# A swapped and negated third row in the table of a Fourier step, and one copy out of PSUM in place of three

## The chip, the cores and the metric

The kernel runs on one core of one Trainium2 chip. Its engines are TensorE (PE in the profile, its weight loads PEld), VectorE (DVE), ScalarE (ACT), GpSimd (POOL) and SyncE (SP, which here only issues DMAs). Each works through its own queue in order. The metric is the time of one launch on the device in microseconds; the median of three runs of the kernel before is 3733.18 us (3731.57 to 3733.58).

## The reference

Two blocks in a row, all in float32. The first is a long convolution, done with Fourier transforms, between two gates:

```python
h_filt = (np.maximum(pos_emb @ w1, 0.0) @ w2) * np.exp(-0.01 * pos)[:, None]
u = x * v                                             # x, v: (4, 12480, 128)
Uf = np.fft.rfft(u, n=2 * S, axis=1)
Hf = np.fft.rfft(h_filt, n=2 * S, axis=0)
y = np.fft.irfft(Uf * Hf[None], n=2 * S, axis=1)[:, :S, :]
x2 = (x * y).reshape(B * S, D)                        # 49920 x 128
```

The second is a layer whose activation is h cos(h):

```python
h = x2 @ w_in                                         # 49920 x 2048
out = (h * np.cos(h)) @ w_out                         # 49920 x 128
```

## The kernel before

The transform of each of the four batches is made of small matrix products, in two steps there (f1, f2) and two back (i1, i2). A sequence is laid out as 104 rows (partitions) by 120 columns, and the columns are folded first: sums of mirrored columns go to places 0 to 59, differences to places 64 to 123. So one column of a pair of channels, called b (64 of them, CB), is a block of 104 partitions by 124 places (KE = 124, ODD = 64).

The first step f1 multiplies this block, as the left operand, with the table c1 (two rows of 96 numbers, a sine and a cosine, of 104 partitions): `f1_mm`, L414 to L417. It does so for each of the two channels i of b, into one PSUM bank of 124 partitions, 2 x 192 numbers each. Partitions 0 to 63 (sums) then hold real and imaginary part in that order. For partitions 64 to 123 (differences) the second transform step wants the two exchanged, and one of them negated. This is done as the results leave PSUM, `f1_evict`, L428 to L435: one copy for partitions 0 to 63 (L431), one copy for the other half's second part (L433), and a negating copy for its first part (the lambdas at L423 and L425). `f1_takers` gives a column b as a whole to ACT or to DVE, by a share. The same step of the filter has its own eviction in five instructions (L437 to L448), since its results go to two tiles.

`units` (L535) drives every step: for each j it calls the matmuls, in two halves, and between the halves takes one `next` of the eviction of the column before. It yields a number of steps, by which the later batches are paced.

The stages, in order of time:

- From 0 to about 64 us: the hidden layer of the filter, and x times v of the first batch (`first_u`: L404 multiplies, L410 sums, on DVE and POOL; the loads L385 go through SP's queue).
- From 64 to 122: f1 of the filter with the eviction `f1_evict_filter`, share 0.53, beside the rest of `first_u` (L895 to L897), then beside `inverse_tables` (L900 to L905): POOL computes arguments (L209 to L226), ACT makes sines of them (L235). These sines lie in ACT's queue between the evictions.
- From 118 to 171: f1 of the first batch, share 0.55 (L922), beside the conversion of w_in (L145 to L168).
- From 171 to 270: f2 of the first batch and the filter at once (`f2_both_units`): ACT and DVE make each table w (L300, L302), PE multiplies, ACT scales the filter's result (L635), which is stored to DRAM (hd).
- Then i1 of the first batch, and from 338 us the main loop (L995 to L1024). It carries the second block tile by tile, 16 chunks c a tile: `moe_up` (PE into "ph", then L755 on ACT and L756 on DVE), `moe_act` (L761 on ACT, L762 on DVE), `moe_sums` on POOL, `moe_down` (L787 on PE). In each chunk `convolve` (L989) pulls as many units of the convolution as it is owed. So i2 of one batch and f1, f2 and i1 of the next, `forward_units` (L713), are woven between the chunks. A tile's begin needs a transposed tile: `moe_turn` (L738) takes one bank for it (PE L136, copied by ACT L744); `moe_back` (L811) transposes results (copied by L818).

In the first part the convolution has eight PSUM banks ("ps"). In the main loop it has two and then three ("cv"), which `moe_turn` shares; "ph" has three, the accumulators two. From the main loop on every matmul with a left operand over 64 columns is cut in two, `tiled` in `mm` (L129 to L132): results for partitions 0 to 63 and from 64 are two instructions, which the profile shows as 104*64 and 104*60. Before that it is one, 104*124. A float32 matmul stands in the trace as two passes, each with its weight load.

Of the kernel before, what the change touches and what calls it, by code (L numbers as in the profile page):

```python
# [9 lines left out]
F32 = mybir.dt.float32  # L10
I32 = mybir.dt.int32
U32 = mybir.dt.uint32
AF = mybir.ActivationFunctionType
ALU = mybir.AluOpType
# [19 lines left out]
def kernel(  # L34
# [46 lines left out]
    nc = tc.nc  # L81
# [4 lines left out]
    N1, N2 = 96, 120  # L86
    R = S // N2
# [3 lines left out]
    ODD = 64  # L91
    KE = ODD + H
# [4 lines left out]
    KF = N1 - 2 * (N2 - N1)  # L97
# [22 lines left out]
    twd = dram.tile([N1, 2, N2], F32, name="twd")  # L120

    const = ctx.enter_context(tc.tile_pool(name="const", bufs=1))
    c1 = const.tile([R, 2, N1], F32, name="c1")
    even = const.tile([KE, 2, N2], F32, name="even")
    tw_w = const.tile([KE, 2, N1], F32, name="tw_w")

# [2 lines left out]
    def mm(dst, left, right, start=True, stop=True):  # L129
        n = dst.shape[0]  # L130
        for lo, hi in ((0, CB), (CB, n)) if tiled[0] else ((0, n),):
            nc.tensor.matmul(dst[lo:hi], left[:, lo:hi], right, start=start, stop=stop)  # L132
# [104 lines left out]
    def forward_tables(pool):  # L237
        t = Tables(pool, nc.vector, 1)
        part = t.whole([P, 1], [[1, 1]], channel_multiplier=1, name="part")
        step = t.whole([P, P], [[1, P]], name="step")  # L240
        step4 = t.whole([P, P], [[4, P]], base=1, name="step4")


        odd_p = t.whole([P, 1], [[1, 1]], base=1, channel_multiplier=2, name="odd_p")
        quarter_p = pool.tile([P, 2], F32, name="quarter_p")
        nc.vector.tensor_scalar(out=quarter_p[:, 0:1], in0=part[:, :], scalar1=float(ODD),
                                scalar2=None, op0=ALU.is_ge)
        nc.vector.scalar_tensor_tensor(
            out=odd_p[:, :], in0=quarter_p[:, 0:1], scalar=-2.0 * ODD, in1=odd_p[:, :],
            op0=ALU.mult, op1=ALU.add)  # L250

        nc.vector.tensor_scalar(out=quarter_p[:, 0:1], in0=quarter_p[:, 0:1],
                                scalar1=-N2 / 2.0, scalar2=N2 / 2.0, op0=ALU.mult, op1=ALU.add)
        nc.vector.tensor_scalar(out=quarter_p[:, 1:2], in0=quarter_p[:, 0:1],
                                scalar1=N2 / 2.0, scalar2=None, op0=ALU.add)
        yield from t.sines(step4, part, 4 * N1, [(c1[:, 0, :], 1), (c1[:, 1, :], 0)])
        yield from t.sines(step, odd_p, 2 * N2,
                           [(even[:, i, :], quarter_p[0:KE, i:i + 1]) for i in range(2)])
        yield from t.sines(step4, odd_p, 2 * TURN, [(tw_w[:, 0, :], 1), (tw_w[:, 1, :], 0)])
# [153 lines left out]

    def f1_mm(ps, u, b, i):  # L414

        mm(ps[0:KE, i * 2 * N1:(i + 1) * 2 * N1], u[:, b, 0:KE, i],
           c1[0:u.shape[0], :, :].rearrange("p r k -> p (r k)"))  # L417

    def f1_takers(b, share):


        if int((b + 1) * share) > int(b * share):
            return nc.scalar.copy, lambda out, in_: nc.scalar.activation(  # L423
                out, in_, AF.Copy, scale=-1.0)
        return nc.vector.tensor_copy, lambda out, in_: nc.vector.tensor_scalar(  # L425
            out=out, in0=in_, scalar1=-1.0, scalar2=None, op0=ALU.mult)

    def f1_evict(ps, b, share):  # L428
        copy, negated = f1_takers(b, share)
        pj = ps[:, 0:4 * N1].rearrange("p (i r k) -> p r k i", i=2, r=2)  # L430
        copy(out=parts[0:ODD, :, :, b, :], in_=pj[0:ODD])  # L431
        yield
        copy(out=parts[ODD:KE, 0, :, b, :], in_=pj[ODD:KE, 1])  # L433
        negated(parts[ODD:KE, 1, :, b, :], pj[ODD:KE, 0])
        yield  # L435

    def f1_evict_filter(ps, b, share):  # L437

        copy, negated = f1_takers(b, share)
        pj = ps[:, 0:4 * N1].rearrange("p (i k) -> p k i", i=2)  # L440
        near, far = ftile[:, b, :, :], above[:, b, :, :]
        copy(out=near[0:ODD], in_=pj[0:ODD, 0:N1 + KF])
        copy(out=far[0:ODD], in_=pj[0:ODD, N1 + KF:])
        yield
        copy(out=near[ODD:KE, 0:N1], in_=pj[ODD:KE, N1:])
        negated(near[ODD:KE, N1:], pj[ODD:KE, 0:KF])
        negated(far[ODD:KE], pj[ODD:KE, KF:N1])
        yield  # L448

    def f2_mm(ps, w, k1, i, filt=False):  # L450
# [84 lines left out]
    def units(n, steps, before, mm, after, parts, ahead=2, skip=0):  # L535


        for j in range(min(ahead, n)):
            for _ in before(j) or ():
                pass  # L540
        yield 0.0
        last = iter(())
        for j in range(n):
            early = iter(before(j + ahead) or () if j + ahead < n else ())
            now = None
            for i in range(parts):
                if i == skip or 2 * (i - skip) == max(parts, 2):
                    now = mm(j, now, int(i > skip))
                if i == 0 and parts == 1:
                    now = mm(j, now, 1)  # L550
                next(last, None)
                next(early, None)
                yield steps / parts
            for _ in early:
                pass
            next(last, None)
            last = after(j, now)
        for _ in last:
            pass
        yield REST  # L560
# [23 lines left out]
            yield from units(H // UA, U_STEPS, before, lambda j, ps, i: None, after, 3,  # L584
                             ahead=bufs - 2)

    def f1_units(bank, u, share=0.5, evict=f1_evict):
        def mm(j, ps, i):
            if i == 0:
                ps = bank()  # L590
            f1_mm(ps, u, j, i)
            return ps

        return units(CB, F1_STEPS, lambda j: None, mm, lambda j, ps: evict(ps, j, share), 2)

    def f2_units(bank):
        with tc.tile_pool(name="there", bufs=3) as pool:
            ws, hs = {}, {}

            def before(j):  # L600
                ws[j] = pool.tile([KE, 2, N2], F32, name="w")
                nc.sync.dma_start(ws[j][:, :, :], wd[j, :, :, :])
                hs[j] = pool.tile([N2, 2, CB, 4], F32, name="h")
                nc.sync.dma_start(hs[j][:, :, :, :], hd[j, :, :, :, :])

            def mm(j, ps, i):
                if i == 0:
                    ps = bank()
                f2_mm(ps, ws[j], 2 * j, i)
                return ps  # L610

            yield from units(N1 // 2, F2_STEPS, before, mm,
                             lambda j, ps: f2_product(pool, ps, hs.pop(j), 2 * j, False), 4)
# [28 lines left out]
    def i1_units(bank):  # L642
        with tc.tile_pool(name="mid", bufs=2) as pool:
            def mm(j, ps, i):
                if i == 0:
                    ps = bank()
                i1_mm(ps, j, i)
                return ps

            yield from units(CB, I1_STEPS, lambda j: None, mm,  # L650
                             lambda j, ps: i1_evict(pool, ps, j), 2)
# [61 lines left out]
    def forward_units(bank, back):  # L713

        f2 = f2_units(bank)
        next(f2)
        yield from f1_units(bank, slots[0:R, :, :, :])
        yield from f2
        next(back)
        yield from i1_units(bank)  # L720
# [114 lines left out]
    with tc.manual_schedule():  # L835
        with tc.tile_pool(name="psum", bufs=8, space=PSUM) as psum, \
                ExitStack() as first:
            def bank():
                return psum.tile([P, BANK], F32, name="ps")

            spool = ctx.enter_context(tc.tile_pool(name="slots", bufs=1))
            slots = spool.tile([P, CB, 2 * N2, 2], F32, name="slots")
            parts = slots[:, :, 0:2 * N1, :].rearrange("p b (r k) i -> p r k b i", r=2)
            above = slots[:, :, 2 * N1:2 * N2, :]
# [6 lines left out]
            with tc.tile_pool(name="layers", bufs=1, side="right") as pool:  # L851
# [16 lines left out]
                window = filter_window(pool)  # L868
                nc.gpsimd.memset(aT[:, 0:H, NCH * ROWS:FR], 0.0)
                sines = forward_tables(pool)  # L870
                peTs = {}
                for i in range(NCH + 1):
# [14 lines left out]
            ftile = fpool.tile([P, CB, N1 + KF, 2], F32, name="ftile")  # L887
            clear_gap(ftile[0:FR, :, :, :])
            with tc.tile_pool(name="out", bufs=1, side="right") as pool:
                for j in range(H // 2):  # L890
                    filter_out(pool, bank, aT, ftile, j, w2_sb)
                    for _ in range(1 + (j % 3 == 0)):
                        next(first_u)
            f1 = f1_units(bank, ftile[0:FR, :, :, :], 0.53, f1_evict_filter)
            for _ in first_u:  # L895
                for _ in range(2):
# [14 lines left out]
            def beside(units, pieces, factor, more=lambda pool: iter(())):  # L911
                with tc.tile_pool(name="convert", bufs=1) as pool:
# [6 lines left out]
                    for _ in [*convert, *other]:  # L919
                        pass  # L920

            beside(f1_units(bank, slots[0:R, :, :, :], 0.55),  # L922
                   [(wind[:, c], w) for c, w in in_pieces], INV_TWO_PI)
            lpool = ctx.enter_context(tc.tile_pool(name="late", bufs=1))
# [130 lines left out]
```

## Time and profile before

| what | value |
|---|---|
| median of the three runs | 3733.18 us |
| span of the profiled execution, first to last instruction | 3730.7 us |
| its own time beyond the span | not recorded; the median of the runs is 2.4 us over the span |
| PE busy, mean granted TensorE clock | 3627.8 us (97%), 0.993 |
| DVE, ACT, POOL busy | 2970.8, 2256.0, 2787.4 us |
| DMA moved | 279.61 MB, mean 75 GB/s |
| f1 matmuls, later batches | 768 of 104*64 and 768 of 104*60 |
| f1 matmuls, first batch and filter | 256 of 104*124 and 256 of 96*124 |
| f1 evictions, later batches | 96 columns on ACT, 96 on DVE, three instructions each |
| f1 evictions, first batch | 35 on ACT, 29 on DVE, three instructions each |
| f1 evictions, filter | 33 on ACT, 31 on DVE, five instructions each |

How to read the lines below. A line of the timeline has the start in us from the span's begin, how long the merged instructions last together, the engine, the line of the code, the operation, output and inputs by tile name, partitions by elements, and how many; in brackets, how long the engine had been idle and which instruction's end released it. A line of the waits has who waited for whom, the sum in us, how often, and the longest. A line of the stretches has the length, then busy us of PE, PEld, DVE, ACT and POOL with the number of instructions, then the granted clock, the DMA share and GB/s. A matmul's duration covers its way through the array, so the next one starts before it ends: pitch is read from starts.

### The profile page before, as it was taken

What the parts mean: (1) busy time and instruction counts of PE and PEld (TensorE: products, weight loads), DVE (VectorE), ACT (ScalarE), POOL (GpSimd) and SP (SyncE); (2) the same over time, 40 slices, a digit from 0 to 9 for tenths busy, and PEclk for the clock granted to TensorE, in tenths of its full rate; (3) what the DMA queues carried; (4) which work ended last, traced back from release to release, by engine and by line L of the source; (5) the groups of instructions that cost most, each with busy time, mean ns of one, the idle gap of its engine ahead of it and who ended that gap; (6) DMA issues with size and microseconds to landing.
All of it is one profiled execution on the core that took longest, in us unless ns stands there. A gap on an engine that the chain in (4) does not pass through costs nothing.

```text
span 3730.7 us, 101448 instructions
## 1 busy us (share of the span) xinstructions
PE 3627.8 (97%) x40298; PEld 2574.6 (69%) x40298; DVE 2970.8 (80%) x5812; ACT 2256.0 (60%) x4660; POOL 2787.4 (75%) x3271
## 2 busy tenths in 40 slices
PE   7898999999999999999999999999999999999999
PEld 6777776666668776766667776666667786666666
DVE  8887887788887777888887777888887757787777
ACT  5756666665554556665555455665565446666666
POOL 7666987578883887588884788578885447887877
PEclk9999999999999999999999999999999999999999
DMA  6263551012221662022210563012220261000000
GB/s 168 62 182 101 162 157 56 15 53 72 71 62 45 164 172 57 13 63 70 73 55 16 152 171 98 19 38 73 73 64 25 73 175 31 19 19 24 19 24 14
DMA packets 209710, 279.61 MB, mean 75 GB/s; under 512 B 17111, under 2 KB 146535, under 8 KB 209111
## 3 DMA queue, kind: packets, MB, share of 16 engines
q1 hardware_dynamic: 209239, 273.12, 26.0%
q8 instruction: 321, 5.26, 0.6%
q14 instruction: 150, 1.23, 0.1%
HBM read 193.64 MB, written 79.42 MB: 73 GB/s over the span
## 4 chain that ended last, share of the span: by engine, by line
PE 83%; DVE 4%; ACT 1%; POOL 1%; issue 1%; DMA 0%; ACTq 0%; POOLq 0%; DVEq 0%
PE ph L132 30%; PE cv L132 21%; PE accb L787 17%; PE acca L787 13%; PE cv L136 1%; DVE gt L762 1%; DVE gt L756 1%; PE ph L136 1%; ACT gt L755 1%; POOL ts L770 0%; ACT at L744 0%; POOL slots L410 0%; ACT tile L818 0%; DVE t L481 0%; DVE xt L404 0%
## 5 line engine op out<-in xcount | busy, mean ns | idle before, releaser
L755 ACT ACTIVATE gt<-ph 128x512 int32<-128x512 f32 (+1 forms) x1380 | 822.3, 596 | 1138.3 <-PE ph L132 1081.7
L770 POOL TENSOR_TENSOR ts<-gt 128x512 f32<-128x512 f32 (+2 forms) x784 | 1005.2, 1282 | 598.5 <-PE accb L787 526.9
L132 PE MATMUL ph<-at,w_in_sb 128*64 128x512 f32 (+1 forms) x5520 | 1428.2, 592 | 14.2 <-ACT tile L818 6.5
L756 DVE SCALAR_TENSOR_TENSOR gt<-ph,gt 128x512 f32<-128x512 f32 (+1 forms) x1380 | 947.6, 687 | 619.7 <-ACT gt L755 608.6
L761 ACT ACTIVATE gt<-gt 128x512 f32<-128x512 f32 (+1 forms) x1568 | 972.1, 620 | 3.5 <-DVE gt L756 2.9
L762 DVE TENSOR_TENSOR gt<-ph,gt 128x512 f32<-128x512 f32 (+1 forms) x1380 | 934.7, 677 | 0.0
L787 PE MATMUL accb<-ts,w_out_sb 128*64 128x128 f32 (+2 forms) x9408 | 649.7, 272 | 0.0
L774 POOL TENSOR_TENSOR ts<-gt,ts 128x256 f32<-128x256 f32 (+2 forms) x784 | 573.8, 732 | 61.5
L773 POOL TENSOR_TENSOR ts<-ts,gt 128x256 f32<-128x256 f32 (+2 forms) x784 | 573.6, 732 | 61.5
L787 PEld LDWEIGHTS acca<-gt,w_out_sb 128*64 128x64 f32 x6272 | 399.3, 137 | 267.1 <-issue 232.2
L787 PEld LDWEIGHTS accb<-ts,w_out_sb 128*64 128x64 f32 x9408 | 543.5, 137 | 0.0
L787 PE MATMUL acca<-gt,w_out_sb 128*64 128x128 f32 (+2 forms) x6272 | 479.2, 272 | 0.0
L787 PEld LDWEIGHTS accb<-gt,w_out_sb 128*64 128x64 f32 x3136 | 225.8, 137 | 253.0 <-issue 199.7
L132 PEld LDWEIGHTS ph<-at,w_in_sb 128*64 128x64 f32 x5520 | 354.0, 137 | 34.6 <-ACT tile L818 14.7
L482 POOL TENSOR_TENSOR slots<-slots,t 120x256 f32<-120x256 f32 x384 | 281.1, 738 | 120.3 <-DVE t L481 72.4
L132 PEld LDWEIGHTS cv<-slots,tm 96*64 96x64 f32 (+1 forms) x3840 | 245.5, 128 | 127.0 <-issue 114.7
L787 PE MATMUL accb<-gt,w_out_sb 128*64 128x128 f32 (+1 forms) x3136 | 311.1, 273 | 4.3 <-DVE ot L808 2.8
L787 PE MATMUL acca<-ts,w_out_sb 128*64 128x128 f32 (+1 forms) x3136 | 308.5, 272 | 1.7 <-POOL ts L773 1.6
L132 PE MATMUL cv<-slots,tm 96*64 96x128 f32 (+1 forms) x3840 | 278.3, 287 | 8.8 <-POOL tm L306 5.6
L132 PEld LDWEIGHTS cv<-cs,slots 120*64 120x64 f32 (+1 forms) x3072 | 167.9, 125 | 61.0 <-issue 59.0
L787 PEld LDWEIGHTS acca<-ts,w_out_sb 128*64 128x64 f32 x3136 | 201.6, 137 | 3.1 <-POOL ts L773 2.9
L132 PEld LDWEIGHTS cv<-c,slots 104*60 104x60 f32 (+1 forms) x1536 | 110.4, 137 | 124.6 <-issue 95.6
(145 smaller groups left out, 4113.5 us busy)
## 6 DMA issues: line engine op xcount, KB each, us to landing
h<-hd SPq DMA_DIRECT2D x144, 240.0 KB
tm<-td SPq DMA_DIRECT2D x96, 312.0 KB
xt<-in_x_dram SPq DMA_DIRECT2D x120, 208.0 KB
vt<-in_v_dram SPq DMA_DIRECT2D x120, 208.0 KB
xs<-in_x_dram SPq DMA_DIRECT2D x120, 208.0 KB
zd<-xs SPq DMA_DIRECT2D x119, 208.0 KB
tile<-zd SPq DMA_DIRECT2D x96, 256.0 KB
w<-wd SPq DMA_DIRECT2D x144, 116.2 KB
```

The lines of the kernel that those rows point to most:

```text
L132: nc.tensor.matmul(dst[lo:hi], left[:, lo:hi], right, start=start, stop=stop)
L136: nc.tensor.transpose(dst, src, ident[0:n, 0:n])
L482: nc.gpsimd.tensor_tensor(y[:, r], y[:, r], t[:, r], op=op)
L755: nc.scalar.activation(turns, ph[:, 0:m], AF.Identity, bias=phase)
L756: nc.vector.scalar_tensor_tensor(out=part, in0=ph[:, 0:m], scalar=phase, in1=turns, op0=ALU.add, op1=ALU.subtract)
L761: nc.scalar.activation(part, part, AF.Sin, scale=scale)
L762: nc.vector.tensor_tensor(part, ph, part, op=ALU.mult)
L770: nc.gpsimd.tensor_tensor(ts[:, 0:2, 0:half], gt[:, :, half:2 * half], gt[:, 0, 0:2 * half].rearrange("p (h n) -> p h n", h=2), op=ALU.sub ...
L773: nc.gpsimd.tensor_tensor(t[2], t[1], b11, op=ALU.add)
L774: nc.gpsimd.tensor_tensor(t[3], b21, t[2], op=ALU.subtract)
L787: nc.tensor.matmul(acc[h * CB:(h + 1) * CB, place, 0:r], w_out_sb[:, pair, weight, :], right[:, h * r:(h + 1) * r], start=(pair == 0 and i ...
```

## The change

The table c1 gets a third row, the negated first one, made once by ACT. The lower half of the places (64 to 123) is multiplied with rows 1 and 2 instead of rows 0 and 1, so its results stand in PSUM already exchanged and negated. For this f1 always cuts its matmul in two at place 64, in the first batch and the filter too. One copy then takes all 124 partitions (two for the filter, which has two target tiles). In the later batches the share goes from 0.5 to 1.0, so every one of these copies is ACT's. The shares of the first batch (0.55) and of the filter (0.53) stay. The eviction now has one `yield` in place of two; the steps that `units` yields are the same.

```diff
-    c1 = const.tile([R, 2, N1], F32, name="c1")
+    c1 = const.tile([R, 3, N1], F32, name="c1")
...
         yield from t.sines(step4, part, 4 * N1, [(c1[:, 0, :], 1), (c1[:, 1, :], 0)])
+        nc.scalar.activation(c1[:, 2, :], c1[:, 0, :], AF.Copy, scale=-1.0)
...
     def f1_mm(ps, u, b, i):
-        mm(ps[0:KE, i * 2 * N1:(i + 1) * 2 * N1], u[:, b, 0:KE, i],
-           c1[0:u.shape[0], :, :].rearrange("p r k -> p (r k)"))
+        dst = ps[:, i * 2 * N1:(i + 1) * 2 * N1]
+        for r, (lo, hi) in enumerate(((0, ODD), (ODD, KE))):
+            nc.tensor.matmul(dst[lo:hi], u[:, b, lo:hi, i],
+                             c1[0:u.shape[0], r:r + 2, :].rearrange("p r k -> p (r k)"),
+                             start=True, stop=True)
...
     def f1_evict(ps, b, share):
-        copy, negated = f1_takers(b, share)
-        pj = ps[:, 0:4 * N1].rearrange("p (i r k) -> p r k i", i=2, r=2)
-        copy(out=parts[0:ODD, :, :, b, :], in_=pj[0:ODD])
+        pj = ps[:, 0:4 * N1].rearrange("p (i k) -> p k i", i=2)
+        taker(b, share)(out=slots[0:KE, b, 0:2 * N1, :], in_=pj[0:KE])
         yield
-        copy(out=parts[ODD:KE, 0, :, b, :], in_=pj[ODD:KE, 1])
-        negated(parts[ODD:KE, 1, :, b, :], pj[ODD:KE, 0])
+
+    def f1_evict_filter(ps, b, share):
+        pj = ps[:, 0:4 * N1].rearrange("p (i k) -> p k i", i=2)
+        copy = taker(b, share)
+        copy(out=ftile[0:KE, b, :, :], in_=pj[0:KE, 0:N1 + KF])
         yield
...
-        copy(out=near[0:ODD], in_=pj[0:ODD, 0:N1 + KF])
-        copy(out=far[0:ODD], in_=pj[0:ODD, N1 + KF:])
-        yield
-        copy(out=near[ODD:KE, 0:N1], in_=pj[ODD:KE, N1:])
-        negated(near[ODD:KE, N1:], pj[ODD:KE, 0:KF])
-        negated(far[ODD:KE], pj[ODD:KE, KF:N1])
+        copy(out=above[0:KE, b, :, :], in_=pj[0:KE, N1 + KF:])
         yield
...
-    def f1_units(bank, u, share=0.5, evict=f1_evict):
+    def f1_units(bank, u, share, evict=f1_evict):
...
-        yield from f1_units(bank, slots[0:R, :, :, :])
+        yield from f1_units(bank, slots[0:R, :, :, :], 1.0)
```

`taker(b, share)` returns ACT's copy or DVE's copy for column b, by the share, as `f1_takers` did.

More of the change, by code (lines that the diff above doesn't have):

```diff
@@ L414, in f1_mm, with taker @@
     def f1_mm(ps, u, b, i):
-        mm(ps[0:KE, i * 2 * N1:(i + 1) * 2 * N1], u[:, b, 0:KE, i],
-           c1[0:u.shape[0], :, :].rearrange("p r k -> p (r k)"))
-    def f1_takers(b, share):
+        dst = ps[:, i * 2 * N1:(i + 1) * 2 * N1]
[3 more added lines that the diff above has]
+                             start=True, stop=True)
+    def taker(b, share):
         if int((b + 1) * share) > int(b * share):
[L423 to L426, printed above, removed]
+            return nc.scalar.copy
+        return nc.vector.tensor_copy
     def f1_evict(ps, b, share):
-        copy, negated = f1_takers(b, share)
-        pj = ps[:, 0:4 * N1].rearrange("p (i r k) -> p r k i", i=2, r=2)
-        copy(out=parts[0:ODD, :, :, b, :], in_=pj[0:ODD])
-        yield
-        copy(out=parts[ODD:KE, 0, :, b, :], in_=pj[ODD:KE, 1])
-        negated(parts[ODD:KE, 1, :, b, :], pj[ODD:KE, 0])
+        pj = ps[:, 0:4 * N1].rearrange("p (i k) -> p k i", i=2)
+        taker(b, share)(out=slots[0:KE, b, 0:2 * N1, :], in_=pj[0:KE])
         yield
     def f1_evict_filter(ps, b, share):
-        copy, negated = f1_takers(b, share)
         pj = ps[:, 0:4 * N1].rearrange("p (i k) -> p k i", i=2)
-        near, far = ftile[:, b, :, :], above[:, b, :, :]
-        copy(out=near[0:ODD], in_=pj[0:ODD, 0:N1 + KF])
-        copy(out=far[0:ODD], in_=pj[0:ODD, N1 + KF:])
+        copy = taker(b, share)
+        copy(out=ftile[0:KE, b, :, :], in_=pj[0:KE, 0:N1 + KF])
         yield
-        copy(out=near[ODD:KE, 0:N1], in_=pj[ODD:KE, N1:])
-        negated(near[ODD:KE, N1:], pj[ODD:KE, 0:KF])
-        negated(far[ODD:KE], pj[ODD:KE, KF:N1])
+        copy(out=above[0:KE, b, :, :], in_=pj[0:KE, N1 + KF:])
         yield
```

## The prediction

> **What bounds the kernel now.** I read the page first, for the balance of the engines and the chain that ended last.
>
> ```profile
> PE 3627.8 (97%) x40298; PEld 2574.6 (69%) x40298; DVE 2970.8 (80%) x5812; ACT 2256.0 (60%) x4660; POOL 2787.4 (75%) x3271
> ...
> PE 83%; DVE 4%; ACT 1%; POOL 1%; issue 1%; DMA 0%; ACTq 0%; POOLq 0%; DVEq 0%
> ```
>
> TensorE is busy for 97% of the span and holds 83% of the chain, so instructions taken off DVE or ACT are worth nothing by themselves. They are worth something only where PE stands still for them. The whole gap is 3730.7 - 3627.8 = 103 us, and the question is which part of it the three-instruction eviction owns. So I read stretches next: the three first steps of later batches, side by side.
>
> ```profile
> 604.00:766.00 162.00, 156.23 (x1695) 111.81 (x1692) 121.27 (x236) 103.70 (x232) 89.81 (x99) 1.00 0.08 21
> 1443.00:1593.00 150.00, 148.93 (x1676) 104.92 (x1674) 120.81 (x236) 103.46 (x232) 89.44 (x99) 1.00 0.07 18
> 2309.00:2460.00 151.00, 149.63 (x1682) 105.36 (x1680) 121.32 (x237) 103.65 (x233) 90.25 (x99) 1.00 0.07 19
> ```
>
> The same 64 columns b take 162 us in the second batch and 150 and 151 in the third and fourth, with equal work (about 1,680 matmuls each). In the last two PE idles for 1.1 and 1.4 us, so nothing is to be had there. In the second batch 12 us are lost. The waits of that stretch and its order in time say how:
>
> ```profile
> PEld cv L132 <- PE cv L132: 9.7, 27, 0.4
> ...
> PE cv L136 <- issue: 4.7, 4, 1.2
> ```
> ```profile
> 641.32 1.11 PE L132 MATMUL cv<-c,slots 104*64 104x192 f32 x8
> ...
> 641.38 0.35 DVE L425 TENSOR_SCALAR slots<-cv 60x192 f32<-60x192 f32 x1
> ...
> 641.85 0.22 PEld L132 LDWEIGHTS cv<-c,slots 104*64 104x64 f32 x4 [0.36 <-PE cv L132]
> ...
> 643.75 0.85 PE L132 MATMUL cv<-c,slots 104*64 104x192 f32 x8
> ```
> ```profile
> 701.26 0.35 DVE L425 TENSOR_SCALAR slots<-cv 60x192 f32<-60x192 f32 x1
> 701.69 0.42 PEld L136 LDWEIGHTS cv<-ident,tile 128*128 128x128 f32 x4 [1.39 <-issue]
> 701.72 0.63 PE L136 MATMUL cv<-ident,tile 128*128 128x128 f32 x4 [1.18 <-issue]
> ```
>
> The view names PE itself and "issue", but each time PE goes on 0.1 us after the negated copy L425 of DVE ends (641.73, then 641.85; 701.61, then 701.69). Both are waits for one of the three "cv" banks: the second half of DVE's eviction comes a step late, behind L756 and L762. Eight matmuls take 1.11 us where they take 0.85 without it.
>
> Then the first batch, which nothing else covers. Its beginning and its end:
>
> ```profile
> 119.93 0.43 POOL L226 TENSOR_TENSOR turned<-moved,turned 96x120 f32<-96x120 f32 x1
> 120.39 0.30 ACT L235 ACTIVATE tw_t<-turned 96x120 f32<-96x120 f32 x1 [1.89 <-POOL turned L226]
> ...
> 121.91 0.68 PE L132 MATMUL ps<-c,slots 104*124 104x192 f32 x1 [7.05 <-ACT slots L423]
> ```
> ```profile
> 170.31 0.33 ACT L423 ACTIVATE slots<-ps 60x192 f32<-60x192 f32 x1
> 170.54 1.77 ACT L300 ACTIVATE ps<-even,tw_w 124x120 f32<-124x120 f32 x6
> ...
> 171.43 1.18 PE L132 MATMUL ps<-slots,w 124*120 124x256 f32 x2 [4.68 <-DVE w L302]
> ```
> ```profile
> 169.00:175.00 6.00, 3.57 (x9) 2.72 (x10) 1.12 (x4) 3.28 (x12) 0.00 (x0) 0.50 0.20 60
> 176.00:182.00 6.00, 6.00 (x29) 4.99 (x28) 5.89 (x14) 3.80 (x11) 3.82 (x6) 1.00 0.55 156
> ```
>
> GpSimd's table chain ends at 120.4; ACT stands behind it and holds a bank, so PE stands still for 7 us. At the end PE is done at 166.75, but ACT still has evictions until 170.54, and f2 cannot start before 171.43. From 169 to 175 the granted clock is 0.50.
>
> **The change, part by part.**
>
> Later batches, f1_evict. Before, a column costs ACT 460 + 313 + 325 ns or DVE 540 + 361 + 353, 96 columns each. After, one ACT copy of 124x384. No such row exists: 64x384 on ACT took 460 ns, 96x240 took 349 and 128x512 took 586 to 592, which lie on one line in the elements whatever the partitions; bounds 460 and 592, and I take 470. DVE loses 96 x 1.25 = 120 us, ACT 105 - 90 = 15. PE's instructions stay: f1_mm was already cut at column 64 there, and only the right operand of the lower half is another. What this brings on PE: 27 x (1.11 - 0.85) = 7.0 us and 4 x 1.18 = 4.7 us in the second batch, 11.7 together, 12 to 13 by the comparison with the other batches. Next late is PE itself: ACT's queue for a step is L755 (597), L761 (622) and the copy (470), 1.69 us in a step that the third batch does in 2.28; the copy waits for matmuls issued earlier, and L755 behind it waits for ph. The bank comes free a step earlier than now. I take 11, and 0.5 for the other two batches (bounds 0 and 2.5, their idle time).
>
> The Trainium skill speaks against this part: "TensorEngine Tiling (Array Packing)", PSUM Bottleneck, advises to use both ScalarE and VectorE for evacuation. The trace has the load that decides, ACT 1.69 of 2.28 us a step; by the rule the third rival below would come instead.
>
> First batch and filter, matmuls. One 104*124 matmul becomes 104*64 and 104*60. Whole, a column's four passes start 0.16 us apart (27 in 4.55 us, the last one 0.33 long), so 0.65 us. Halved, in later batches, eight take 0.85, of which the last 0.33 overlaps what follows, and the next column's pitch is again 0.65; the two halves' loads (137 ns each) appear as pairs in 0.17 us, so they overlap. With different right operands there is L787, which does twelve 128-column matmuls in 0.85. I take no cost; the other end is four loads one after the other, 0.55 us a call (first slower rival). Negating c1 costs one 104x96 ACT instruction; the nearest, 60x96, took 0.24 us, at 14 us of the span where ACT is not on the path: nothing, 0.3 if uncovered.
>
> First batch and filter, evictions. ACT 1.11 us a column becomes 0.47, DVE 1.26 becomes 0.55 (filter: 392 + 232 and 450 + 240 stay, three each go). What it brings:
> (a) ACT's eviction after the last sine (five instructions, 120.72 to 121.86) is two, so PE goes on 0.5 us earlier.
> (b) GpSimd's chain can start earlier. It waited 0.7 us for DVE's L410 at 97.6 and 2.0 us for vt loads, and SP's queue, where a vt load stands behind an xt load, waited 16.9 us for DVE's L410, which is queued between evictions. I take 2.0 of the 2.7. The rest of that stage gains nothing: it ends with GpSimd.
> (c) From 121.9 to 166.75 PE does 252 passes: 41.0 us at 0.1625, and 3 more at half clock until 127.8, so 0.9 us are waits. They go.
> (d) At the end the gap of 4.68 becomes one copy (0.5) and L300, L302 (0.9), 1.5 us: 3.2.
> (e) With a gap of 1.5 us the clock should not fall. A gap of 2.35 us at 600.6 left the clock at 1.00, one of 3.05 at 269.7 was followed by 0.50 (275 to 278), as were those of 4.68 and 7.05. f2's first passes ran 4.2 us at 0.50, which is 2.1 lost.
> Together 0.5 + 2.0 + 0.9 + 3.2 + 2.1 = 8.7; bounds 4 (without b and e) and 11. Everything behind it is chained and moves with it; f2 in this stage is paced by its stores, whose first issue moves by the same.
>
> The Trainium skill, "TensorE: Matmul & The Clock Gate", Part 1, gives an idle window of some 3.4 us for the fall to half clock. By it (e) holds; a trace with a gap over that would take the 2.1 back.
>
> Sum: 8.7 + 11 + 0.5 = 20.2 off the span of 3730.7. The median of the three runs, 3733.18, lies 2.4 us above the span, and I leave that around it: 3730.7 - 20.2 + 2.4 = **3713 us**.
>
> **The rivals.**
> 1. The bank wait is replaced: ACT's single copy lies behind L755 and L761, and PE waits for it as it did for DVE. For: ACT is a strict queue. Against: the ACT-evicted columns show no such wait now, though they cost 1.10 us. Only the first batch gains: 3733 - 9 = 3724.
> 2. The first batch's gain is swallowed because GpSimd or the stores of f2 pace it: 3733 - 11.5 = 3721.5.
> 3. ACT becomes the bound at tile borders. Four times a batch L744 (586) and L818 (592) join a step: 1.69 + 1.18 = 2.87 against 2.28, 0.6 late, x 12 = 7 us: 3720.
> 4. Slower: in the untiled stages the halves run one after the other on the weight path, 4 x 137 ns = 0.55 us a call and 1.1 us a column instead of 0.65. The first batch takes 70 + 3 us instead of 45, so f2 starts about 25 later less 2; the filter takes 70 + 3 from 64.2 and ends at 137, 15 past the gate; less 11 in the second batch: 3733 + 27 = 3760. It turns slower from about 0.85 us a column. Against: the pairs in later batches. For: no row has halves in this stage.
> 5. No change: DVE's relief and the moved waits cancel, 3733.
>
> **How the numbers follow.** Forecast 0.68 (3705 to 3720), rivals 1 to 3 together 0.17, rival 5 0.08, rival 4 0.07. The low end takes the upper bounds, 11 + 13 + 2.5, and one half-clock window of 3.4 us less (1.7): 3705. The high end is rival 1 with the first batch near the middle of its bounds (6): 3727. What a measurement can tell from no change is about 0.2%, 7.5 us: faster 0.83, same 0.10, slower 0.07.
>
> **What would show it.** Right: the second batch's first step takes 150 to 152 us with no 27-fold bank wait and no 1.18 us ahead of L136; the gap before f2 is under 2 us and the clock there 1.00; f1 copies of 124x384 take about 470 ns; the first batch's passes still start 0.16 apart. Wrong: PEld near 100% in the first f1, new waits of PE for ACT's copies, or L755 late behind them.

## The result and the profile after

The changed kernel takes 3712.35 us (median of 4 runs, 3709.91 to 3713.82) against 3733.38 for the kernel before: a ratio of 0.9945, with a 95% interval of 0.9931 to 0.9959. The prediction was 3713, faster. The profiled execution has a span of 3710.0 us, 20.7 less than before.

In the changed kernel the line numbers have moved: f1's matmul is L419, its copy L431, the filter's copies L438 and L440, the second block's chain L748, L749, L754, L755 and L780 (before: L755, L756, L761, L762, L787), the w table L301 and L303 (before: L300, L302).

First the balance, from the page after, and the new copy, from the groups by form (busy us, mean ns):

```profile
PE 3620.5 (98%) x40810; PEld 2565.9 (69%) x40810; DVE 2823.2 (76%) x5373; ACT 2201.2 (59%) x4396; POOL 2792.2 (75%) x3271
```
```profile
L431 ACT COPY slots<-cv 124x384 f32<-124x384 f32 x192 | 90.8, 473 | 0.0
```

DVE lost 148 us and ACT 55, but the span only 20.7: most of that work lay under PE. The copy of 124 partitions takes 473 ns, as the line through the rows of fewer partitions gave it (470).

Then the first steps of the second, third and fourth batch, as stretches:

```profile
599.00:750.00 151.00, 151.00 (x1706) 109.73 (x1708) 86.86 (x143) 99.34 (x203) 90.16 (x99) 1.00 0.08 23
1426.00:1575.00 149.00, 148.85 (x1678) 105.56 (x1676) 87.16 (x143) 98.58 (x201) 89.60 (x99) 1.00 0.06 18
2291.00:2440.00 149.00, 148.85 (x1680) 105.58 (x1678) 87.05 (x143) 98.69 (x201) 89.50 (x99) 1.00 0.07 18
```

And the longest waits of the first of these, where before there were 27 of PEld for "PE cv" and 4 of PE ahead of L136:

```profile
DVE gt L749 <- ACT gt L748: 64.9, 60, 4.1
POOL ts L763 <- PE accb L780: 54.8, 31, 2.9
ACT gt L748 <- PE ph L132: 49.9, 63, 4.3
PEld cv L419 <- issue: 32.7, 118, 0.3
ACT at L737 <- PE cv L136: 2.5, 4, 0.6
```

The second batch's step has come down from 162.9 us (first to last matmul) to 151.0, and the bank waits are out of the list. In this stretch DVE and ACT now wait for PE, not PE for them.

The first batch is the other place. Its begin in the timeline of ACT and that of PE, and its end:

```profile
118.76 0.30 ACT L235 ACTIVATE tw_t<-turned 96x120 f32<-96x120 f32 x1 [1.90 <-POOL turned L226]
```
```profile
110.22 2.80 PE L419 MATMUL ps<-c,slots 104*64 104x192 f32 x32
119.54 5.70 PE L419 MATMUL ps<-c,slots 104*64 104x192 f32 x34 [6.52 <-ACT slots L440]
```
```profile
162.05 0.48 ACT L431 COPY slots<-ps 124x384 f32<-124x384 f32 x1 [0.82 <-PE ps L419]
162.43 1.78 ACT L301 ACTIVATE ps<-even,tw_w 124x120 f32<-124x120 f32 x6
163.93 1.09 DVE L303 SCALAR_TENSOR_TENSOR w<-even,tw_w,ps 124x120 f32<-124x120 f32 x4 [1.96 <-ACT ps L301]
164.00 0.34 SPq L919 DMA_DIRECT2D cs<-csd  x1
164.32 1.21 PE L132 MATMUL ps<-slots,w 124*120 124x256 f32 x2 [2.32 <-DVE w L303]
```

GpSimd's chain sets ACT free 1.6 us sooner, and PE goes on at 119.54 instead of 121.91. ACT has no backlog at the end: its last copy starts at 162.05 and f2 at 164.32, not 171.43.

Where the 20.7 us came from, by the first matmul of each stage (us from the span's begin):

| stage begins | before | after | gained so far |
|---|---|---|---|
| f2 of the first batch | 171.43 | 164.32 | 7.1 |
| i1 of the first batch | 272.77 | 266.39 | 6.4 |
| main loop | 338.32 | 333.15 | 5.2 |
| f1 of the second batch | 602.99 | 598.22 | 4.8 |
| f2 of the second batch | 770.97 | 754.33 | 16.6 |
| f1 of the third batch | 1442.89 | 1426.04 | 16.8 |
| f2 of the third batch | 1600.17 | 1581.58 | 18.6 |
| f2 of the fourth batch | 2466.99 | 2446.47 | 20.5 |
| end | 3730.7 | 3710.0 | 20.7 |

So the second batch's first step gave 11.9, the third's and fourth's 3.8 together, and the first batch 7.1, of which 2.3 were lost again before the second batch began.

The rows ahead of the second batch hold for this pair of profiles only. Later runs that leave these stages as in the kernel before (unsplit, share_only, late_only) or as in the changed kernel (after_again, one_copy_half, and whole_mm with its whole matmuls) show how much they vary. With the old evictions, in four profiles, f2 of the first batch begins at 171.2 to 172.0 us and f1 of the second batch at 602.3 to 604.1. With the new ones, also in four, they begin at 161.9 to 165.9 and at 593.2 to 598.2. The later stages vary far less: from f2 of the second batch to the end, the eight profiles with the changed kernel's later stages agree within 0.7 us (2955.6 to 2956.3).

### The profile page after: what moved, and what is told of

It reads as the page before. It is cut to its first block, busy times and chain, and to the rows that moved or that the text cites. A ratio compares the mean times of both kernels' runs of the same rounds, so it can differ in the third digit from the quotient of the medians.

```text
span 3710.0 us, 101707 instructions
## 1 busy us (share of the span) xinstructions
PE 3620.5 (98%) x40810; PEld 2565.9 (69%) x40810; DVE 2823.2 (76%) x5373; ACT 2201.2 (59%) x4396; POOL 2792.2 (75%) x3271
## 4 chain that ended last, share of the span: by engine, by line
PE 84%; DVE 4%; ACT 1%; POOL 1%; issue 1%; DMA 0%; ACTq 0%; POOLq 0%; DVEq 0%; SPq 0%
PE ph L132 30%; PE cv L132 18%; PE accb L780 17%; PE acca L780 13%; PE cv L419 3%; PE cv L136 1%; DVE gt L755 1%; DVE gt L749 1%; PE ph L136 1%; ACT gt L748 1%; POOL ts L763 0%; DVE xt L405 0%; POOL slots L411 0%; ACT tile L811 0%; DVE t L474 0%
## 5 line engine op out<-in xcount | busy, mean ns | idle before, releaser
L748 ACT ACTIVATE gt<-ph 128x512 int32<-128x512 f32 (+1 forms) x1380 | 823.0, 596 | 1147.4 <-PE ph L132 1085.7
L749 DVE SCALAR_TENSOR_TENSOR gt<-ph,gt 128x512 f32<-128x512 f32 (+1 forms) x1380 | 949.1, 688 | 718.5 <-ACT gt L748 715.6
L754 ACT ACTIVATE gt<-gt 128x512 f32<-128x512 f32 (+1 forms) x1568 | 971.7, 620 | 3.6 <-DVE gt L749 2.9
L755 DVE TENSOR_TENSOR gt<-ph,gt 128x512 f32<-128x512 f32 (+1 forms) x1380 | 936.5, 679 | 0.0
L780 PE MATMUL accb<-ts,w_out_sb 128*64 128x128 f32 (+2 forms) x9408 | 649.2, 272 | 0.0
L780 PEld LDWEIGHTS acca<-gt,w_out_sb 128*64 128x64 f32 x6272 | 398.4, 137 | 268.1 <-issue 231.7
L780 PEld LDWEIGHTS accb<-ts,w_out_sb 128*64 128x64 f32 x9408 | 543.0, 137 | 0.0
L780 PE MATMUL acca<-gt,w_out_sb 128*64 128x128 f32 (+2 forms) x6272 | 479.0, 272 | 0.0
L780 PEld LDWEIGHTS accb<-gt,w_out_sb 128*64 128x64 f32 x3136 | 224.6, 137 | 254.9 <-issue 198.7
L780 PE MATMUL accb<-gt,w_out_sb 128*64 128x128 f32 (+1 forms) x3136 | 310.6, 273 | 4.5 <-DVE ot L801 2.9
L780 PE MATMUL acca<-ts,w_out_sb 128*64 128x128 f32 (+1 forms) x3136 | 308.3, 272 | 1.5 <-POOL ts L766 1.2
L780 PEld LDWEIGHTS acca<-ts,w_out_sb 128*64 128x64 f32 x3136 | 201.0, 137 | 3.0 <-POOL ts L766 2.7
L132 PE MATMUL cv<-slots,w 124*56 124x256 f32 (+1 forms) x1152 | 190.7, 407 | 1.9 <-ACT at L737 1.9
```

The costliest lines, as they stand in the source:

```text
L748: nc.scalar.activation(turns, ph[:, 0:m], AF.Identity, bias=phase)
L749: nc.vector.scalar_tensor_tensor(out=part, in0=ph[:, 0:m], scalar=phase, in1=turns, op0=ALU.add, op1=ALU.subtract)
L754: nc.scalar.activation(part, part, AF.Sin, scale=scale)
L755: nc.vector.tensor_tensor(part, ph, part, op=ALU.mult)
L780: nc.tensor.matmul(acc[h * CB:(h + 1) * CB, place, 0:r], w_out_sb[:, pair, weight, :], right[:, h * r:(h + 1) * r], start=(pair == 0 and i ...
```

## The experiments

The theory is the prediction's: PE stood still for PSUM banks, held by the half of an eviction that comes a step late, and by ACT's backlog in the first batch. The rivals in the later batches: it was fewer instructions, or work taken off DVE, or the share alone. Kernels of one group ran on one chip beside the kernel before; the ratios are to that.

### Later batches: issue the halves together

```diff
         copy(out=parts[0:ODD, :, :, b, :], in_=pj[0:ODD])
-        yield
         copy(out=parts[ODD:KE, 0, :, b, :], in_=pj[ODD:KE, 1])
```

> The kernel before, with the yield between the two halves of f1_evict taken out: a column's three instructions are issued together, half a unit pair earlier for the last two; the same instructions, engines and shares. Theory (a bank is held by the half that comes a step late): the first step of the second batch falls from 163 us to 151 to 155, the 27 waits and the four stops of 1.2 us ahead of L136 go, and the whole is 3719 to 3724. Rival (what helped was fewer instructions, or work taken off DVE): both stay, 3733. A third outcome, L756 late behind 1.1 us of eviction on DVE: waits of PE for DVE gt L762, 3733 or more.

3721.11 us, ratio 0.9970 (0.9959 to 0.9981): as the theory had it. With the same instructions on the same engines the second batch's step is 151 us, in the stretch view:

```profile
604.00:755.00 151.00, 150.60 (x1692) 109.21 (x1694) 120.31 (x235) 103.71 (x231) 90.74 (x100) 1.00 0.08 23
1432.00:1582.00 150.00, 148.90 (x1673) 104.82 (x1670) 121.22 (x237) 103.33 (x231) 89.96 (x99) 1.00 0.07 18
```

DVE is as busy as before (120 us), and yet PE loses almost nothing in the second batch. Fewer instructions and less work on DVE are out as the cause of that gain. The third batch stays at 150.

The trace of the kernel before also shows why only the second batch lost so much. One column on DVE, first in the second batch, then in the third:

```profile
643.45 0.54 DVE L431 COPY slots<-cv 64x384 f32<-64x384 f32 x1
644.61 0.69 DVE L756 SCALAR_TENSOR_TENSOR gt<-ph,gt 128x512 f32<-128x512 f32 x1 [0.62 <-ACT gt L755]
645.22 0.68 DVE L762 TENSOR_TENSOR gt<-ph,gt 128x512 f32<-128x512 f32 x1
645.91 0.36 DVE L433 COPY slots<-cv 60x192 f32<-60x192 f32 x1
646.19 0.35 DVE L425 TENSOR_SCALAR slots<-cv 60x192 f32<-60x192 f32 x1
```
```profile
1470.52 0.54 DVE L431 COPY slots<-cv 64x384 f32<-64x384 f32 x1
1471.07 0.36 DVE L433 COPY slots<-cv 60x192 f32<-60x192 f32 x1
1471.35 0.35 DVE L425 TENSOR_SCALAR slots<-cv 60x192 f32<-60x192 f32 x1
```

From L431 to L433 DVE takes 1.82 to 4.63 us, start to start, in the 32 columns of the second batch, and 0.55 or 0.56 in all those of the third and fourth. There both halves already fell into one chunk of the second block. So this experiment gives the second batch what the other two had.

### Later batches: the share alone

```diff
-        yield from f1_units(bank, slots[0:R, :, :, :])
+        yield from f1_units(bank, slots[0:R, :, :, :], 1.0)
```

> The kernel before, with the share of the later batches at 1.0 and nothing else: three instructions a column, all on ACT. Theory: the half that comes a step late stays, and ACT has 0.60 + 0.62 + 1.02 = 2.24 us of a step of 2.28, over it at tile borders; the second batch's first step stays at 160 us or more, the third and fourth grow from 150 to 151 to 156, the whole is 3733 to 3748. Rival (the gain is the move off DVE, by the share): 3717 to 3720, as DVE loses its 120 us all the same.

3719.46 us, ratio 0.9968 (0.9955 to 0.9981). This expectation failed, on both counts. ACT was busy for 136 of 152 us and kept up, and the bank waits went although the second half still comes a step late. The timeline shows why:

```profile
640.87 0.62 ACT L761 ACTIVATE gt<-gt 128x512 f32<-128x512 f32 x1
...
641.51 0.32 ACT L433 COPY slots<-cv 60x192 f32<-60x192 f32 x1
641.61 0.68 DVE L762 TENSOR_TENSOR gt<-ph,gt 128x512 f32<-128x512 f32 x1
...
641.73 0.33 ACT L423 ACTIVATE slots<-cv 60x192 f32<-60x192 f32 x1
...
642.26 0.82 PE L132 MATMUL cv<-c,slots 104*64 104x192 f32 x8
```

On ACT the late half stands behind L761, which ends at 641.49, and the bank is free at 642.06, before PE's next column. On DVE it would stand behind L762, which waits for L761 and ends at 642.29; 0.63 us of copies (353 ns started 281 after the other) would end it at 642.92. The column needs the bank for its second four matmuls, about 642.6. (The DVE case is worked out, not run.) So the theory has to be narrower: the wait was a late half *in DVE's queue, behind L762*. It goes if the half is issued earlier (unsplit) or if another queue takes it (here).

### Later batches: one copy, on both engines

```diff
-        yield from f1_units(bank, slots[0:R, :, :, :], 1.0)
+        yield from f1_units(bank, slots[0:R, :, :, :], 0.5)
```

> The changed kernel with the share of the later batches back at 0.5: one copy a column, half of them on DVE (about 0.55 us each). Theory (the bank comes free in time because there is one copy in the first half): first steps of 151, 149 and 149 us as with the change, whole 3710 to 3715. Rival (the gain needs DVE free): the second batch's first step goes back by half of its 12 us or more, 3718 to 3724.

3709.73 us, ratio 0.9940 (0.9924 to 0.9957), not to be told from the changed kernel. Stretches:

```profile
594.00:745.00 151.00, 150.86 (x1698) 109.24 (x1698) 101.87 (x174) 87.20 (x170) 90.63 (x100) 1.00 0.08 23
1421.00:1570.00 149.00, 148.80 (x1674) 112.13 (x1671) 101.43 (x175) 86.72 (x169) 89.67 (x99) 1.00 0.06 16
```

The time is 0.3 us under the range expected. With one copy the share is free: 151 and 149 us either way. The change cured the bank wait twice over, by the single copy and by the move to ACT, and each would have done for the second batch.

### The change in the later batches alone

```diff
...
+        if not tiled[0]:
+            nc.tensor.matmul(dst[0:KE], u[:, b, 0:KE, i],
+                             c1[0:u.shape[0], 0:2, :].rearrange("p r k -> p (r k)"),
+                             start=True, stop=True)
+            return
         for r, (lo, hi) in enumerate(((0, ODD), (ODD, KE))):
...
```

Filter and first batch keep their old evictions.

> The change in the later batches alone; filter and first batch keep whole matmuls and the three and five instructions. Theory: the two traces put 4.8 us of the gain before the second batch's first step and 15.9 behind its begin, so this gives 3733.4 - 15.9 = 3717.5 (3716 to 3719), with f2 at 171 us of the span as before. Rival (the first stages' gain is lost again behind them, or the parts hang together): 3712 or 3722 and more.

3716.99 us, ratio 0.9960 (0.9945 to 0.9975): 15.0 us under the kernel before, against 15.9 expected. f2 of the first batch begins at 171.15 as before. The changed kernel's two measurements lie 21.0 and 21.6 us under the kernel before, so 6.0 to 6.6 are left for the first stages, against 4.8 in the pair of profiles. Within the spread of the runs the parts add up.

### First stages: whole matmuls again

The same edit of the matmul as in the last experiment, on the changed kernel with its single copies. The kernel so leaves out the exchange and negation of the lower half in these two stages.

> The changed kernel, but the matmuls of the filter and the first batch are whole again (104*124, rows 0 and 1 of the table for all places); so the lower half's exchange and negation are left out in these two stages, and all else is as in the changed kernel. Theory (halves run beside each other and cost nothing): 3710 to 3714 like the changed kernel, passes 0.16 us apart in both. Rival (halving has a price on the weight path): the first step of the first batch is shorter by several us and the whole 3709 or less.

3709.65 us, ratio 0.9939 (0.9923 to 0.9956), no difference from the changed kernel (3711.11 and 3712.35 in its two measurements, runs from 3708.8 to 3712.9 here and 3709.7 to 3713.8 there). The median is 0.35 us under the range expected, so the time alone doesn't tell it from the rival. The timeline of PE settles it, whole first and then the changed kernel:

```profile
127.70 22.59 PE L419 MATMUL ps<-c,slots 104*124 104x192 f32 x138
```
```profile
127.71 22.59 PE L419 MATMUL ps<-c,slots 104*64 104x192 f32 x276
```

138 whole passes and 276 halves, with different right operands, take the same 22.59 us: some 0.163 us a pass or a pair. The whole step agrees. From its stop to its end PE took 41.26 us here and 42.46 in the changed kernel, of which 4.10 and 6.64 at a granted clock of 0.50. Counted half, these leave 39.21 and 39.14 us for 240 passes or pairs. So the difference lies in the clock and not in the halves.

### What sets the begin of f2

In the profile after, L303 waited until 163.93, though ACT's first term stood at 162.80. The load of cs went out at 164.00, and the waits of SP's queue say for what:

```profile
SPq L919 <- DMA wind<-power: 1.5, 1, 1.5
```

It is the last store of the converted w_in: both cs and w lie in the memory of the conversion. Two experiments. The first makes the first w ahead, in the memory of cs:

```diff
...
+            cs = lpool.tile([KE, 2, N2], F32, name="cs")
+            for i in range(2):
+                make_w(cs[:, i, :], i, half=bank)
             beside(f1_units(bank, slots[0:R, :, :, :], 0.55),
...
             def before(j):
...
+                if j == 4:
+                    nc.sync.dma_start(cs[0:N2, :, :], csd[:, :, :])
+                if j == 0:
+                    ws[j] = cs
...
```

> The changed kernel, with the first table w of f2 made ahead of the first batch's first step, in the memory that later holds cs (whose load moves behind the fourth table). Theory (with the evictions gone, the start of f2 waits for DVE's L303, and that for the last store of the converted weights, which lands 1.3 us after ACT's last copy is done): the gap of PE ahead of f2 falls from 2.3 to 1 us or less, the clock does not fall there, and the whole is 1.5 to 4 us under the changed kernel, 3708 to 3711. Rival (f2 is paced by its stores or by the second table anyway): 3712.

3711.62 us, ratio 0.9940 (0.9925 to 0.9955): not in the range expected, and not to be told from the changed kernel. The gap fell to 0.63 us and the clock stayed up there. In PE's timeline, where f2's first matmuls now read w from cs:

```profile
109.19 1.52 PE L419 MATMUL ps<-c,slots 104*64 104x192 f32 x16
118.41 1.86 PE L419 MATMUL ps<-c,slots 104*64 104x192 f32 x10 [7.70 <-ACT slots L440]
...
162.83 0.67 PE L132 MATMUL ps<-slots,cs 124*120 124x256 f32 x2 [0.63 <-ACT slots L431]
```

f2 began 1.5 us sooner, but f1 had already begun 1.0 sooner (109.19 against 110.22), so the step itself is only 0.5 us shorter. PE got two columns ahead of its stop, not four, and the stop is 7.70 us instead of 6.52: the two terms of w hold two banks behind ACT's sines. Most of what was gained at the end was lost at the begin. The second stores sooner (`every` is 13 in this step), and holds no bank:

```diff
...
-                        if i % 14 == 0:
+                        if i % every == 0:
...
```

> The changed kernel, with the pieces of w_in converted at every 13th unit of the first batch's first step instead of every 14th, so that the last store is issued about 3 us sooner; nothing else. Theory (DVE's first L303 waits for that store's landing, as w lies in the memory of the conversion): the gap of PE ahead of f2 falls from 2.3 to 1.3 to 1.7 us, what the prediction gave it; the whole 1 to 3 us under the changed kernel, by the clock's fall there or not. Rival (L303 waits for ACT alone): the gap stays at 2.3.

3710.33 us, ratio 0.9939 (0.9924 to 0.9954); the changed kernel beside it had 3711.11. The whole is inconclusive, 0.8 us apart in spreads of 3 to 4. The gap is not, in the timeline:

```profile
161.09 0.48 ACT L431 COPY slots<-ps 124x384 f32<-124x384 f32 x1 [0.82 <-PE ps L419]
161.32 0.34 SPq L919 DMA_DIRECT2D cs<-csd  x1
161.46 1.79 ACT L301 ACTIVATE ps<-even,tw_w 124x120 f32<-124x120 f32 x6
161.93 1.12 DVE L303 SCALAR_TENSOR_TENSOR w<-even,tw_w,ps 124x120 f32<-124x120 f32 x4 [0.94 <-ACT ps L301]
162.33 0.70 PE L132 MATMUL ps<-slots,w 124*120 124x256 f32 x2 [1.29 <-DVE w L303]
```

L303 now follows L301 by half a microsecond, and the gap is 1.29 us instead of 2.32. So the store is shown to be what L303 waited for.

### What holds PE at 113 us

```diff
                 for i, _ in enumerate(f1):
-                    if i % 5 == 0:
+                    if i % 7 == 0:
                         next(sines, None)
```

> The changed kernel, with the inverse tables' sines taken after every seventh unit of the filter's first step instead of every fifth, so that they lie later in ACT's queue. Theory (PE's stop of 6.5 us ahead of the first batch is ACT standing behind GpSimd's table chain, with banks held): the stop falls under 2 us, f2 starts 4 to 6 us earlier, and the whole is 3706 to 3709. Rival (the chain itself is what the first batch needs, or it is held up in turn by ACT's later sines): the stop only moves, 3712.

3704.92 us, ratio 0.9924 (0.9909 to 0.9938), the best of all. PE's timeline:

```profile
108.11 6.05 PE L419 MATMUL ps<-c,slots 104*64 104x192 f32 x72
117.38 2.99 PE L419 MATMUL ps<-c,slots 104*64 104x192 f32 x20 [3.21 <-ACT slots L431]
```

Nine columns are done ahead of the stop instead of four, and the stop is 3.21 us, not 6.52. It does not fall under 2 as expected, since all of the last sines still come before the first batch's copies. f2 begins at 158.0, 6.3 us sooner, and the whole is 1 us under the range expected. Not all of the 6.3 is the edit's: the filter's first step had begun 2.2 us sooner (62.23 against 64.42) with nothing changed ahead of it. The edit shows in the first batch's f1, 49.9 us from its begin to f2 where it was 54.1.

The two edits were also put together with it:

> Both of the edits before, the first w ahead and the sines after every seventh unit, on the changed kernel. Theory: the two stops are apart and the gains add, 3702 to 3707. Rival (one thing sets the begin of f2 in both, such as the stores of the converted weights): no better than the better of the two.

3708.64 us, ratio 0.9934 (0.9919 to 0.9949): worse than the sines alone. In its profile PE got six columns ahead of a stop of 5.74 us, as the terms of w again hold banks behind the sines, and f1 takes 51.8 us where the sines alone have 49.9. The rest of the 3.7 us is not traced to a cause.

> The sines after every seventh unit and the pieces at every 13th, on the changed kernel. Theory: the two stops are apart, and this one holds no more banks (as the first w made ahead did), so it is 0 to 3 us under the sines alone, 3702 to 3705. Rival: the gap ahead of f2 stays, 3705 or more.

3706.98 us, ratio 0.9932 (0.9916 to 0.9949), beside the changed kernel:

> The changed kernel once more, as the measure for the two beside it: 3709 to 3714. If the half-clock windows of the first 360 us explain its spread (spans of 3707.8 to 3710.5 so far), the parts from 338 us on last as long as in the first profile, and only the parts ahead differ.

3711.11 us (3709.68 to 3712.80), ratio 0.9943 (0.9928 to 0.9958). The gap ahead of f2 was 1.30 in sines_7_store, but the whole no better than the sines alone, which ran on another chip; the expected 0 to 3 did not come. Its timeline has a stop that the sines alone do not have:

```profile
123.90 34.34 PE L419 MATMUL ps<-c,slots 104*64 104x192 f32 x400 [1.85 <-DVE slots L431]
```

PE waits there for a copy on DVE, 1.85 us, which is more than the gap gave. That DVE is late because it converts sooner is likely, but not shown. Of the versions tried, sines_7 has the shortest time: 28 us under the kernel before, which ran beside it, and 6 to 7 under the changed one, which ran on other chips.

The expectation on the spread held in part. Between the two profiles of the changed kernel the stretch from i1 of the second batch (1090 us) to the end lasts the same to 0.2 us. The early stages shift: the filter's first step began at 64.42 and 66.46, with nothing changed. But the second batch's first step too, 151.0 and 152.7, with the clock at half from 598.6 to 602.0 in the second profile. So the half clock reaches behind the first 360 us.

## Why the prediction was right

The mechanism was right: bank waits in the second batch, and ACT's backlog in the first. That the sum, 20.2, met 20.7 to half a microsecond is luck, since errors of some 4 us cancelled. Step by step:

- **Second batch, 11 (11.7 by its rows).** Measured 11.9. By the starts of the columns, every second column gained 0.23 to 0.26 us and the four tile borders 1.1 to 1.25 each, as the two waits had been read. The mechanism was right in its place. Why DVE's half came late was told right too (behind L762), but not that this order decides and not the number of copies; share_only showed it.
- **Third and fourth batch, 0.5.** Measured 3.8. The idle time of PE (1.1 and 1.4) was taken as all there was to have, with 2.5 as bound. Each batch gained 0.31 at each of its four tile borders and 0.5 between f1's end and f2, and the fourth some 0.3 at its begin. So idle time of PE, whose ends are modelled, understated what there was to gain. It is not the late half's doing: from f1's to f2's begin these batches take 157.3 and 157.6 us in unsplit, as in the kernel before, but 156.0 and 156.3 in share_only and 155.8 in one_copy_half.
- **ACT as the bound (rival 3) and the bank wait on ACT (rival 1).** Neither came; even with three instructions a column on ACT (share_only) the second batch's step stays at 152 us.
- **Halves cost nothing (against rival 4).** Shown by the pair of 22.59 us.
- **(a) and (b), 2.5.** Measured 2.4: the chain 1.6 sooner, the rest by fewer instructions after the last sine. The waits moved as told: from 55 to 98 us SP's queue waited 16.9 us for DVE's sums (L410) before and 2.4 after, and GpSimd's 2.0 for vt loads became 0.3.
- **(c), 0.9.** PE's run from the stop to the end fell from 44.8 to 42.5 us. Beyond the waits it has three columns less to do, 2.0 us, because PE now runs four columns ahead of the stop, not one. The prediction had missed this gain; 0.4 us more at half clock (6.64 us of it where it was 5.91) took a little back.
- **(d), 3.2.** Measured 2.4: the gap became 2.32, not 1.5. What was late next was the landing of the last store, which the prediction did not name; store_sooner gave 1.29. The prediction's own sign, a gap under 2 us with the clock at 1.00, did not come.
- **(e), 2.1.** It failed in the profiled execution, where the clock stood at 0.50 after the gap, and came in another kernel with the same gap. The stretches of the changed kernel, then of one_copy_half, whose gap was 2.31:

```profile
164.50:170.00 5.50, 5.50 (x13) 4.09 (x14) 2.30 (x7) 1.13 (x3) 0.00 (x0) 0.50 0.24 69
171.00:176.00 5.00, 5.00 (x25) 4.14 (x24) 4.81 (x12) 3.41 (x9) 3.31 (x6) 1.00 0.52 155
267.00:273.00 6.00, 6.00 (x31) 5.94 (x31) 1.66 (x5) 1.78 (x5) 0.93 (x4) 0.50 0.74 229
```
```profile
164.00:171.00 7.00, 6.94 (x31) 5.52 (x32) 4.35 (x13) 3.41 (x9) 1.57 (x3) 1.00 0.36 105
```

In the first, 13 matmuls run in 5.5 us where 25 run in 5.0 later; i1 too began at 0.50, from 267 to 273, where the kernel before had 275 to 278. f2 lasted 0.7 us longer than before and i1 1.2, which is most of what was lost again before the second batch. That the clock is the cause of these 1.9 us is not shown. For i1 the other profiles speak for it: it took 66.8 us in both profiles with 6.8 us of half clock there, and 65.5 to 66.5 in the eleven others. For f2 they do not: in the six profiles without half clock in f2 it took between 100.6 and 103.2 us, and in the changed kernel's 102.1.

So in this pair of profiles the first batch came to 4.8 where 8.7 was said, and the later batches to 15.9 where 11.5 was said. The first figure is uncertain: by the whole times it is 6.0 to 6.6, and over the four profiles each of old and new first stages the means of the second batch's begin lie 7.7 us apart. The second is firm, as late_only has 15.0.

## What to carry to other kernels

A wait that the profile puts down to the waiting engine itself, or to nothing ("issue"), is worth laying beside the timeline: if it ends each time just after one engine's last copy out of a bank, it may be a bank wait, and an edit that only moves that copy tells. What holds the bank is the last piece of an eviction, so one copy, issuing the pieces together, or a queue whose work ahead of it ends sooner, may each be enough, whatever the load of the engines. Where a stage's end moves up, look for what else had been landing under its cover: here a store, whose memory the next stage takes over.

## What the runs showed of the hardware

A gap of PE of 2.3 us is on the edge of the clock's fall. After the gap ahead of f2 the clock fell for 6.8 us in one profile of the changed kernel and 3.4 us in whole_mm, and not in one_copy_half or in the changed kernel's second profile, with gaps of 2.30 to 2.32. Ahead of the second batch's f1 a gap of 2.35 or 2.36 was followed by half clock in 3 of 13 profiles. Gaps of 1.29, 1.30 and 0.63 ahead of f2 were not followed by it in the four profiles that have them, that of 2.68 in sines_7 was, and those of 4.68 to 4.71 were in all four. A longer gap is no certain sign either: those of 3.04 to 3.06 ahead of i1 were followed by half clock in 12 of 13 profiles, and not in share_only, and in sines_7_store one of 3.21 at 115.4 left the clock at 1.00 until 123.8, when it fell behind a gap of 1.85. The Trainium skill, "TensorE: Matmul & The Clock Gate", Part 1, gives a free-running window of about 3.4 us and an idle window for the fall; the lengths of 3.4 and 6.8 us agree with it, but a gap well under a window was enough here.

With that, and a filter step that began anywhere from 62.2 to 66.5 us in these profiles for reasons not traced, the runs of one kernel lie 2 to 6 us apart. Edits worth 1 us in the first stages can't be told by the whole time, only by their place in the profile.
